# Batch 1's key-value products one block of w_out later, its v released later, its first q transposes one block sooner, and half of batch 2's maximum tree moved into tile 1

## The chip, the cores and the metric

The kernel runs on one core of one Trainium2 chip. A core has TensorE (PE in the profile; its weight loads are listed apart as PEld), VectorE (DVE), ScalarE (ACT), GpSimd (POOL) and SyncE (SP), which here only issues DMAs. Each engine works through its own instructions in order; engines wait for one another, and for DMAs, on semaphores. The metric is the device time of one execution in microseconds (us). Lower is better.

## The reference, cut to what matters

```python
# q, k, v: (8 batches, 8 heads, 576 positions, 64); float32
q_s = exp(q - max(q, axis=-1));  q_s /= sum(q_s, axis=-1)      # over the head's 64
k_s = exp(k - max(k, axis=2));   k_s /= sum(k_s, axis=2)       # over the 576 positions
kv  = einsum('bhsd,bhse->bhde', k_s, v)                        # 64x64 for each head
x   = einsum('bhsd,bhde->bhse', q_s, kv)                       # then to (4608 tokens, 512)
h   = x @ w_in                                                 # 512 -> 2048
out = maximum(0.01 * h, h) @ w_out                             # 2048 -> 512
```

There is no product of q with k: attention here is two softmaxes and two small products. Nearly all the arithmetic lies in the two dense layers behind it.

## The kernel before

**Tiles.** The 4608 tokens are cut into nine tiles of 512 columns. `xT` holds the attention's result, channels on partitions, tokens along columns. A batch has 576 tokens, so tile 0 needs batch 0 alone, and tile 1 needs the last 64 tokens of batch 0 and the first 448 of batch 1, and so on. In each tile layer 1 (`layer1`, L511) makes 16 blocks `ph` of 128 hidden channels, ScalarE applies the leaky rectifier to each (`leaky`, L520, into `gj`), and layer 2 (`layer2`, L532) accumulates 16 products into each of four `pout` blocks, which are copied to `out_sb` and stored by SP (L526, L529). In tile 0 layer 2 goes block of w_out by block of w_out: for each j of 16, four matmuls, one for each of the four 128-token groups. In later tiles it goes token group by token group.

**The attention of the next batches lies between these matmuls.** The order is written by hand. `at(t, u, fns)` hangs functions on hook u of tile t; `run(t, u)` emits them there. In tile 0, hooks 0 to 31 come in pairs behind the leaky rectifiers of layer 1, and hook 32 + j comes behind the four layer-2 matmuls of w_out block j. In a later tile, hook j comes behind the rectifier of block j, and hook 16 + 4g + i behind the fourth, eighth, twelfth and sixteenth matmul of token group g. A hook settles where an instruction stands in its own engine's queue and nothing more; between engines only the semaphores count.

**One batch's steps**, each with its line in the profile:

- k: a maximum over the nine positions that a partition holds, in four steps on VectorE (`k_tree`, L151; H0 and H1 are the two halves of the four head rows); the maximum over partitions by transposes on VectorE (`k_allmax`, L156 to L176); the subtraction (`k_sub`, L184); the exponential on ScalarE into `ke` (`k_exp`, L192).
- v: a cast to bf16 `vb` (`v_cast`, L202 on ScalarE, L204 on GpSimd).
- q: maximum (L215), subtraction (L274, on GpSimd or VectorE), exponential on ScalarE (L282), sum, reciprocal and scaling on VectorE (L291, L293, L298). Batch 1's q is turned by transposes on TensorE, seven positions of one half at a time (`q_turn_first`, L254, into `psum_q`), and ScalarE copies each to `qT` (`q_keep_first`, L267). From batch 2 on a DMA turns it (`q_turn`, L504).
- the 72 small matmuls of k with v (`kv`, L311, into two `pkv` buffers), their scaling on VectorE (`kd_make`, L330 and L331, into `kd`), and the product of q with the result (`cross`, L430, into `po`), which is copied into `xT` (L453, L499 for batch 1's `attend_next`).

**PSUM.** One pool, `psB`, has six buffers, and `ph`, `pkv`, `psum_q`, `psum_qt`, `po` and two of tile 0's four `pout` blocks share them. A new tile takes a buffer that is free in program order, and its first matmul waits for the last reader of the old one.

**Loads.** SP issues all loads of q, k and v, in program order, and waits on semaphores in that order too. Two small devices hold it back. `hold_sync` (L563) loads a few bytes from a weight, so that what SP issues later comes behind that weight's landing. In `more_loads` ScalarE writes one element into batch 1's v tile (L637), so that SP may issue the load of v only once ScalarE has come that far. The weights w_in and w_out are loaded from GpSimd's queue, w_out's blocks 2 to 15 in seven pieces.

```python
    def more_loads():
        st[1]["v"] = t = raw("v_raw")
        nc.scalar.copy(out=t[0:1, 0, 0, 0:1], in_=identf[0:1, 0:1])
        load(v, 1, "v_raw", [(H0, ALLR), (H1, ALLR)], t)
        hold_sync(1, w_out_sb[0:1, 11, 0:128])
```

Of the kernel before, what the change touches and what calls it, by code (L numbers as in the profile page):

```python
# [25 lines left out]
def kernel(  # L26
# [9 lines left out]
    nc = tc.nc  # L36
# [95 lines left out]
    def k_begin(b):  # L132
        st[b]["ke"] = ke_pool.tile([P, R, HL, D], BF16, name="ke")
        st[b]["kmax"] = mx_pool.tile([P, HL, D], FP32, name="kmax")
        st[b]["kmaxT"] = mx_pool.tile([P, HL * D], FP32, name="kmaxT")
        st[b]["kall"] = mx_pool.tile([P, HL, D], FP32, name="kall")

    def k_tree(b, hs, steps=slice(0, 4)):
        n = hs.stop - hs.start
        ks = st[b]["k"][:, hs]  # L140
        if steps.start == 0:
            st[b]["t4"] = mx_pool.tile([P, HL, 4, D], FP32, name="t4")[:, 0:n]
        t4 = st[b]["t4"]
        t2, t1 = t4[:, :, 0:2], t4[:, :, 0]
        for o, i0, i1 in (
            (t4, ks[:, :, 0:4], ks[:, :, 4:8]),
            (t2, t2, t4[:, :, 2:4]),
            (t1, t1, t4[:, :, 1]),
            (st[b]["kmax"][:, hs], t1, ks[:, :, 8]),
        )[steps]:  # L150
            nc.vector.tensor_tensor(out=o, in0=i0, in1=i1, op=ALU.max)  # L151
# [29 lines left out]
    def k_sub(eng, b, hs):  # L181
        ks = st[b]["k"][:, hs]
        n = hs.stop - hs.start
        eng.tensor_tensor(  # L184
            out=ks,
            in0=ks,
            in1=st[b]["kall"][:, hs].unsqueeze(2).to_broadcast([P, n, R, D]),
            op=ALU.subtract,
        )
# [17 lines left out]
    def q_begin(b):  # L207
        st[b]["qe"] = qe_pool.tile([P, R, HL, D], BF16, name="qe")
        if b < 2:
            st[b]["qT"] = qT_pool.tile([P, NB, R, L], BF16, name="qT", tag="qT")  # L210
# [39 lines left out]
    def q_turn_first(b, gg, rs=RA):  # L250
        n = rs.stop - rs.start
        ps = psB_pool.tile([P, 2, n, L], BF16, name="psum_q2", tag=BANK_TAG)
        for r in range(n):
            nc.tensor.matmul(  # L254
                ps[:, :, r],
                lhsT=st[b]["qe"][:, rs.start + r, 2 * gg : 2 * gg + 2].rearrange("p h d -> p (h d)"),
                rhs=ident,
                is_transpose=True,
                start=(r == 0),
                stop=(r == n - 1),  # L260
            )
        st[b]["ps2", gg] = ps

    def q_keep_first(eng, b, gg, rs=RA):
        o, i = st[b]["qT"][:, gg::2, rs], st[b]["ps2", gg]
        if eng is nc.scalar:
            eng.copy(out=o, in_=i)  # L267
        else:
            eng.tensor_copy(out=o, in_=i)
# [11 lines left out]
    def q_exp(b, rs, hs=ALLH):  # L281
        nc.scalar.activation(  # L282
            out=st[b]["qe"][:, rs, hs].rearrange("p r h d -> p h r d"),
            in_=st[b]["q"][:, hs, rs],
            func=AF.Exp,
        )

    def q_sum(b, rs, hs=ALLH):
        n, m = rs.stop - rs.start, hs.stop - hs.start
        qsum = small_pool.tile([P, n, HL], FP32, name="qsum")[:, :, 0:m]  # L290
        nc.vector.reduce_sum(out=qsum, in_=st[b]["qe"][:, rs, hs], axis=AX.X)  # L291
        st[b]["qrec", rs.start, hs.start] = qrec = small_pool.tile([P, n, HL], FP32, name="qrec")[:, :, 0:m]
        nc.vector.reciprocal(out=qrec, in_=qsum)  # L293

    def q_norm(b, rs, hs=ALLH):
        n, m = rs.stop - rs.start, hs.stop - hs.start
        qes = st[b]["qe"][:, rs, hs]
        nc.vector.tensor_tensor(  # L298
            out=qes,
            in0=qes,  # L300
            in1=st[b]["qrec", rs.start, hs.start].unsqueeze(3).to_broadcast([P, n, m, D]),
            op=ALU.mult,
        )


    def kv_quads(b, gg, outs, rs=ALLR):
        for r in range(R)[rs]:
            for hp in range(2):
                for hh in range(2):
                    rows = slice(hh * L, (hh + 1) * L)  # L310
                    nc.tensor.matmul(  # L311
                        outs[hh][hp * D : (hp + 1) * D, 0 : D + 1],
                        lhsT=st[b]["ke"][rows, r, 2 * gg + hp],
                        rhs=vb2[b % 2][rows, r, gg, hp, 0 : D + 1],
                        start=(r == 0),
                        stop=(r == R - 1),
                    )

    def kv(b, order=(0, 1)):

        pkv = [psB_pool.tile([P, 2, D + 2], FP32, name="pkv", tag=BANK_TAG) for _ in range(2)]
        for gg in order:
            kv_quads(b, gg, [pkv[hh][:, gg] for hh in range(2)])
        st[b]["pkv"] = pkv

    def kd_make(b):
        for hh in range(2):
            pkv = st[b]["pkv"][hh]
            krec = small_pool.tile([P, 2, 1], FP32, name="krec")
            nc.vector.reciprocal(out=krec, in_=pkv[:, :, D : D + 1])  # L330
            nc.vector.tensor_tensor(  # L331
                out=kd2[b % 2][:, :, hh],
                in0=pkv[:, :, 0:D],
                in1=krec.to_broadcast([P, 2, D]),
                op=ALU.mult,
            )
# [62 lines left out]
    def q_transpose(b, r0, n, pool=psB_pool, tag=BANK_TAG):  # L399
        ps = pool.tile([P, NB, n, L], BF16, name="psum_qt", tag=tag)  # L400
        for rr in range(n):
            for gg in range(2):
                nc.tensor.matmul(  # L403
                    ps[:, gg::2, rr],
                    lhsT=st[b]["qe"][:, r0 + rr, 2 * gg : 2 * gg + 2].rearrange(
                        "p h d -> p (h d)"
                    ),
                    rhs=ident,
                    is_transpose=True,
                    start=(rr == 0 and gg == 0),  # L410
                    stop=(rr == n - 1 and gg == 1),
                )
        st[b]["ps", r0] = ps

    def q_keep(eng, b, r0, n, gs=slice(0, 4)):
        o, i = st[b]["qT"][:, gs, r0 : r0 + n], st[b]["ps", r0][:, gs]
        if eng is nc.scalar:
            eng.copy(out=o, in_=i)
        else:
            eng.tensor_copy(out=o, in_=i)  # L420
# [122 lines left out]
    def at(t, u, *fns):  # L543
        while t > 0 and u >= 32:
            t, u = t + 1, u - 32
        hooks.setdefault((t, u), []).extend(fns)
# [5 lines left out]
    H0, H1 = slice(0, 2), slice(2, 4)  # L552
# [74 lines left out]
    R7, RE = slice(0, 7), slice(7, R)  # L627
# [21 lines left out]
    at(0, 20, lambda: q_max(1, R7, H0), lambda: q_sub(nc.gpsimd, 1, R7, H0), lambda: k_allmax(1))  # L649
    at(0, 20, lambda: q_max(1, R7, H1), lambda: q_sub(nc.gpsimd, 1, R7, H1), lambda: k_sub(nc.vector, 1, H1))  # L650
    at(0, 20, lambda: k_sub(nc.gpsimd, 1, H0))
    at(0, 25, more_loads)
    at(0, 31, lambda: q_exp(1, R7, H0), lambda: q_sum(1, R7, H0), lambda: q_norm(1, R7, H0))
    at(0, 31, lambda: k_exp(1, H1))
    at(0, 32, lambda: q_exp(1, R7, H1), lambda: q_sum(1, R7, H1), lambda: q_norm(1, R7, H1))
    at(0, 32, lambda: q_sum(0, R3), lambda: q_norm(0, R3))
    at(0, 32, lambda: v_cast(nc.scalar, 1, 0), lambda: v_cast(nc.scalar, 1, 1), lambda: k_exp(1, H0))
    at(0, 42, lambda: q_turn_first(1, 0, R7), lambda: q_keep_first(nc.scalar, 1, 0, R7))
    at(0, 43, lambda: kv(1, (1, 0)), lambda: kd_make(1))
    at(0, 44, lambda: q_turn_first(1, 1, R7), lambda: q_keep_first(nc.scalar, 1, 1, R7))  # L660
    at(0, 44, lambda: q_transpose(0, 8, 1), lambda: q_keep(nc.scalar, 0, 8, 1))
    at(0, 45, lambda: k_begin(2), lambda: q_begin(2), lambda: k_tree(2, H0))
    at(0, 46, attend_next)
    at(1, 0, lambda: q_max(1, RE), lambda: q_sub(nc.gpsimd, 1, RE))
    at(1, 5, lambda: q_exp(1, RE))
# [4 lines left out]

    def plan2():
        b = 2
        at(1, 0, lambda: k_tree(b, H1))
        at(1, 3, lambda: q_max(b, XR[0]), lambda: q_sub(nc.gpsimd, b, XR[0]))
        at(1, 3, lambda: k_allmax(b), lambda: k_sub(nc.vector, b, H0), lambda: k_sub(nc.vector, b, H1))
        at(1, 6, lambda: q_max(b, XR[1]), lambda: q_sub(nc.gpsimd, b, XR[1]))
        at(1, 11, lambda: q_exp(b, XR[0]), lambda: q_sum(b, XR[0]), lambda: q_norm(b, XR[0]))
        at(1, 13, lambda: v_cast(nc.gpsimd, b, 0), lambda: v_cast(nc.gpsimd, b, 1))
        at(1, 14, lambda: q_sum(1, RE), lambda: q_norm(1, RE))
        at(1, 15, lambda: k_exp(b, ALLH), lambda: q_turn(b, XR[0]))  # L680
        at(1, 16, lambda: q_exp(b, XR[1]), lambda: q_sum(b, XR[1]), lambda: q_norm(b, XR[1]))
        at(1, 17, lambda: q_turn(b, XR[1]))
        at(1, 17, lambda: load_all(4))
        at(1, 23, lambda: kv(b))
        at(1, 24, lambda: kd_make(b))
        at(1, 27, lambda: attend_all(b, (XR[0],)), lambda: attend_all(1, (RE,)))
        at(2, 19, lambda: attend_all(b, (XR[1],)))
# [28 lines left out]
    for t in range(3, B - 1):  # L716
        b = t + 1
# [140 lines left out]
```

## Time and profile before

| what | value |
|---|---|
| time, median of 3 runs | 283.06 us (282.93 to 283.38) |
| profiled execution: its own time | 282.68 us |
| profiled execution: span, first to last instruction | 280.9 us |
| granted TensorE clock | 0.998 |
| PE busy | 274.5 us, 98% of the span |
| ACT busy, DVE busy, POOL busy | 161.8, 159.3, 53.4 us |
| bytes moved by DMA | 45.81 MB, mean 163 GB/s |

How to read it: the span is what the engines' instructions cover; the profiled execution's own time has 1.8 us more around it. An engine's busy share over the span says little of a single stage. The chain that ended last tells which engine the end followed, and a timeline of one engine tells when each instruction began, how long it took and what ended an idle stretch before it. A PE row's duration is that of a pipelined instruction and reaches into the next one; the step from one matmul to the next is read from the chain of waits.

### The profile page before, as it was taken

To read this page: it belongs to the slowest core of one execution; us is meant where nothing else is said; L and a number is where in the kernel's file an instruction comes from. 1 tells how busy PE (TensorE), PEld (TensorE's weight loads), DVE (VectorE), ACT (ScalarE), POOL (GpSimd) and SP (SyncE) were. 2 spreads that over 40 slices of the span, in tenths; PEclk is the share of its full clock that TensorE was granted. 3 is DMA by queue.
4 is the path that set the end of the run, shared out by engine and by line. 5 is a ranking of instruction groups with operands and counts; after the bars stand their busy time and mean duration, and the time that the engine had idled before them with its cause. 6 is when DMAs were issued, how large, how long until landed. Compare 5 with 4: busy or idle time off the path is not lost.

```text
span 280.9 us, 5008 instructions
## 1 busy us (share of the span) xinstructions
PE 274.5 (98%) x2022; PEld 133.1 (47%) x2022; DVE 159.3 (57%) x225; ACT 161.8 (58%) x286; POOL 53.4 (19%) x52
## 2 busy tenths in 40 slices
PE   8899999999999999999999999999999999999994
PEld 2378645444444544444444444444444444444443
DVE  2975898999999939966895598644600000000021
ACT  4987575793589276755586448644844364146400
POOL 2847380457013006000400070000000000000000
PEclk9999999999999999999999999999999999999999
DMA  7999999895890696089309930333033300330033
GB/s 243 334 208 317 263 222 392 295 365 194 276 389 18 146 395 204 1 241 400 100 2 279 384 77 0 84 77 74 5 84 75 71 6 0 75 77 0 0 75 77
DMA packets 37207, 45.81 MB, mean 163 GB/s; under 512 B 16064, under 2 KB 20416, under 8 KB 37184
## 3 DMA queue, kind: packets, MB, share of 16 engines
q1 hardware_dynamic: 33696, 41.16, 45.9%
q0 software_dynamic: 3328, 4.20, 8.5%
q8 instruction: 16, 0.26, 0.4%
q10 hardware_dynamic: 160, 0.13, 0.1%
q14 instruction: 7, 0.06, 0.1%
HBM read 36.70 MB, written 9.44 MB: 164 GB/s over the span
## 4 chain that ended last, share of the span: by engine, by line
PE 92%; DVE 3%; DMA 2%; ACT 1%; issue 0%; SPq 0%
PE pout L532 45%; PE ph L511 43%; DMA k_raw<-in_k_dram 2%; PE po L430 2%; DVE t L151 1%; PE pokv L311 1%; PE pkv L311 1%; DVE qe L298 0%; DVE qsum L291 0%; DVE k_raw L380 0%; ACT vb L202 0%; PE psum_q L254 0%; ACT ke L192 0%; PE psum_qt L403 0%; ACT qe L282 0%
## 5 line engine op out<-in xcount | busy, mean ns | idle before, releaser
L532 PE MATMUL pout<-w_out_sb,gj 128*128 128x512 bf16 (+2 forms) x592 | 128.1, 373 | 0.0
L511 PE MATMUL ph<-xT,w_in_sb 128*128 128x512 bf16 (+1 forms) x640 | 126.7, 358 | 0.0
L520 ACT ACTIVATE gj<-ph 128x512 bf16<-128x512 f32 x144 | 82.2, 600 | 26.4 <-PE ph L511 26.1
L511 PEld LDWEIGHTS <-w_in_sb 128*128 128x128 bf16 x640 | 62.3, 98 | 62.2 <-issue 0.2
L532 PEld LDWEIGHTS <-gj 128*128 128x128 bf16 x592 | 56.4, 98 | 64.7 <-issue 0.2
L526 ACT COPY out_sb<-pout 128x512 f32<-128x512 f32 (+1 forms) x29 | 16.8, 579 | 66.0 <-PE pout L532 43.8
L526 DVE COPY out_sb<-pout 128x512 f32<-128x512 f32 (+1 forms) x8 | 4.8, 636 | 70.8 <-PE pout L532 70.8
L204 POOL CAST vb<-v_raw 128x1152 bf16<-128x1152 f32 x13 | 24.4, 1901 | 81.2 <-DMA v_raw<-in_v_dram 58.2
L291 DVE TENSOR_REDUCE qsum<-qe 128x36 f32<-128x2304 bf16 (+5 forms) x13 | 20.0, 1542 | 10.2 <-ACT qe L282 10.1
L192 ACT ACTIVATE ke<-k_raw 128x2304 bf16<-128x2304 f32 (+2 forms) x11 | 17.6, 1597 | 9.5 <-DVE k_raw L184 9.4
L298 DVE TENSOR_TENSOR qe<-qe,qrec 128x2304 bf16<-128x2304 bf16 (+5 forms) x13 | 22.4, 1724 | 0.5
L215 DVE TENSOR_REDUCE qmax<-q_raw 128x36 f32<-128x2304 f32 (+5 forms) x13 | 20.0, 1536 | 0.7 <-DMA q_raw<-in_q_dram 0.7
L282 ACT ACTIVATE qe<-q_raw 128x2304 bf16<-128x2304 f32 (+5 forms) x13 | 17.1, 1317 | 2.4 <-POOL q_raw L274 2.4
L184 DVE TENSOR_TENSOR k_raw<-k_raw,kall 128x2304 f32<-128x2304 f32 (+1 forms) x8 | 17.2, 2163 | 0.3
L453 ACT CAST xT<-po 128x512 bf16<-128x512 f32 (+3 forms) x35 | 15.7, 536 | 1.6 <-PE po L430 1.6
L274 POOL TENSOR_TENSOR q_raw<-q_raw,qmax 128x512 f32<-128x512 f32 (+3 forms) x7 | 12.2, 1736 | 22.1 <-DMA q_raw<-in_q_dram 9.7
L151 DVE TENSOR_TENSOR t<-t 128x256 f32<-128x256 f32 (+2 forms) x22 | 14.7, 669 | 0.7
L151 DVE TENSOR_TENSOR t<-k_raw 128x512 f32<-128x512 f32 (+1 forms) x11 | 13.1, 1188 | 3.0 <-DMA k_raw<-in_k_dram 2.7
L330 DVE RECIPROCAL krec<-pokv 128x2 f32<-128x2 f32 x8 | 1.3, 165 | 22.1 <-PE pokv L430 22.1
L274 DVE TENSOR_TENSOR q_raw<-q_raw,qmax 128x2304 f32<-128x2304 f32 (+1 forms) x6 | 13.2, 2203 | 0.6 <-issue 0.5
L342 PE MATMUL pout<-zero 128*128 128x512 bf16 x24 | 8.8, 510 | 1.3 <-POOL zero L99 1.3
L311 PEld LDWEIGHTS <-ke 64*64 64x64 bf16 x576 | 6.7, 107 | 4.2 <-issue 2.5
(65 smaller groups left out, 107.0 us busy)
## 6 DMA issues: line engine op xcount, KB each, us to landing
out_dram<-out_sb SPq DMA_DIRECT2D x70, 128.0 KB, 2.6
q_raw<-in_q_dram SPq DMA_DIRECT2D x6, 1152.0 KB, 8.4
v_raw<-in_v_dram SPq DMA_DIRECT2D x6, 1152.0 KB, 11.2
k_raw<-in_k_dram SPq DMA_DIRECT2D x5, 1152.0 KB, 6.1
k_raw<-in_k_dram SPq DMA_DIRECT2D x6, 576.0 KB, 6.0
v_raw<-in_v_dram SPq DMA_DIRECT2D x4, 576.0 KB, 7.7
w_in_sb<-in_moe_w_in_dram POOLq DMA_DIRECT2D x8, 256.0 KB, 7.4
w_out_sb<-in_moe_w_out_dram POOLq DMA_DIRECT2D x8, 256.0 KB, 11.6
```

The lines of the kernel that those rows point to most:

```text
L151: nc.vector.tensor_tensor(out=o, in0=i0, in1=i1, op=ALU.max)
L184: eng.tensor_tensor(out=ks, in0=ks, in1=st[b]["kall"][:, hs].unsqueeze(2).to_broadcast([P, n, R, D]), op=ALU.subtract,)
L192: nc.scalar.activation(out=st[b]["ke"][:, :, hs].rearrange("p r h d -> p h r d"), in_=st[b]["k"][:, hs], func=AF.Exp,)
L204: eng.tensor_copy(out=o, in_=i)
L215: nc.vector.tensor_reduce(out=o, in_=st[b]["q"][:, hs, rs], axis=AX.X, op=ALU.max)
L274: eng.tensor_tensor(out=qs, in0=qs, in1=st[b]["qmax", rs.start, hs.start].unsqueeze(3).to_broadcast([P, m, n, D]), op=ALU.subtract,)
L291: nc.vector.reduce_sum(out=qsum, in_=st[b]["qe"][:, rs, hs], axis=AX.X)
L298: nc.vector.tensor_tensor(out=qes, in0=qes, in1=st[b]["qrec", rs.start, hs.start].unsqueeze(3).to_broadcast([P, n, m, D]), op=ALU.mult,)
L511: nc.tensor.matmul(ph, lhsT=w_in_sb[:, cb, j * P : (j + 1) * P], rhs=xT[:, cb, c0 : c0 + n], start=(cb == 0 and first), stop=(cb == NB - 1 ...
L520: nc.scalar.activation(out=o, in_=ph, func=AF.Prelu, alpha=LEAKY_SLOPE)
L526: copy(out=out_sb, in_=pout)
L532: nc.tensor.matmul(pout, lhsT=g_sb[j // 2][:, j % 2, tsub * P : (tsub + 1) * P], rhs=w_out_sb[:, j, os], start=(j == 0), stop=(j == NF - 1),)
```

## The change

Six lines of the plan change; no function does. The numbers in `at(0, 32 + j, ...)` are places behind w_out block j of tile 0.

- The hook of `more_loads` goes from 25 to 27, which is one pair of layer-1 blocks later in ScalarE's queue.
- `q_turn_first(1, 0, R7)`, the first transposes of batch 1's q with their copy, go from behind w_out block 10 to behind block 9.
- `kv(1, (1, 0))` and `kd_make(1)` go from behind block 11 to behind block 12, and there behind the second transposes and the one of batch 0's last position.
- `k_begin(2)`, `q_begin(2)` and `k_tree(2, H0)` go from behind block 13 of tile 0 to hook 0 of tile 1, behind batch 1's `q_max` and just ahead of `k_tree(2, H1)`.

```diff
-    at(0, 25, more_loads)
+    at(0, 27, more_loads)
...
-    at(0, 42, lambda: q_turn_first(1, 0, R7), lambda: q_keep_first(nc.scalar, 1, 0, R7))
-    at(0, 43, lambda: kv(1, (1, 0)), lambda: kd_make(1))
+    at(0, 41, lambda: q_turn_first(1, 0, R7), lambda: q_keep_first(nc.scalar, 1, 0, R7))
     at(0, 44, lambda: q_turn_first(1, 1, R7), lambda: q_keep_first(nc.scalar, 1, 1, R7))
-    at(0, 44, lambda: q_transpose(0, 8, 1), lambda: q_keep(nc.scalar, 0, 8, 1))
-    at(0, 45, lambda: k_begin(2), lambda: q_begin(2), lambda: k_tree(2, H0))
+    at(0, 44, lambda: q_transpose(0, 8, 1), lambda: kv(1, (1, 0)), lambda: q_keep(nc.scalar, 0, 8, 1), lambda: kd_make(1))
     at(0, 46, attend_next)
...
     def plan2():
         b = 2
-        at(1, 0, lambda: k_tree(b, H1))
+        at(1, 0, lambda: k_begin(b), lambda: q_begin(b), lambda: k_tree(b, H0), lambda: k_tree(b, H1))
```

The instructions of every engine stay the same in kind and number; SP's and GpSimd's keep their order.

## The prediction

> **What bounds the kernel.** I read the page's busy table first, then the chain of waits, then the timelines of ScalarE, SP, VectorE and TensorE around the four edits.
>
> ```profile
> PE 274.5 (98%) x2022; PEld 133.1 (47%) x2022; DVE 159.3 (57%) x225; ACT 161.8 (58%) x286; POOL 53.4 (19%) x52
> ```
>
> TensorE is busy for 98% of the span, and from 31.09 us to 277.15 us the chain of waits holds its matmuls alone. So a saving on another engine shortens nothing, and a wait that TensorE takes on in between lengthens the run by its full length. The chain over the stage that the change rearranges:
>
> ```profile
> 40.58 0.39 PE psum_q L254 x7
> 40.97 0.86 PE pout L532 x4
> 41.84 0.71 PE pkv L311 x70
> 42.55 0.97 PE pout L532 x4
> 43.52 0.39 PE psum_q L254 x7
> 43.91 0.11 PE psum_qt L403 x2
> 44.02 1.73 PE pout L532 x8
> 45.75 0.57 PE po L430 x16
> 46.31 0.97 PE pout L532 x4
> 47.28 13.81 PE ph L511 x64
> ```
>
> The last line gives the pace without a wait: 13.81 / 64 = 0.216 us a matmul, 0.863 for a block of four. All layer-2 pieces here keep it, but for 0.11 us more behind each group of small matmuls. So there is no stall to recover. What feeds this stage is ScalarE's queue, and ahead of it SP's load of batch 1's v:
>
> ```profile
> 29.00 0.17 ACT L637 COPY v_raw<-identf 1x1 f32<-1x1 f32 x1
> 29.38 0.60 ACT L520 ACTIVATE gj<-ph 128x512 bf16<-128x512 f32 x1 [0.21 <-PE ph L511]
> ...
> 39.70 1.15 ACT L202 CAST vb<-v_raw 128x1152 bf16<-128x1152 f32 x1 [0.28 <-DMA v_raw<-in_v_dram]
> 40.86 1.16 ACT L192 ACTIVATE ke<-k_raw 128x1152 bf16<-128x1152 f32 x1
> 41.93 0.89 ACT L267 COPY qT<-psum_q 128x896 bf16<-128x896 bf16 x1
> ```
>
> ```profile
> 29.20 0.89 SPq L81 DMA_DIRECT2D v_raw<-in_v_dram x2
> ```
>
> ScalarE waits for v's second half, which lands at 39.68 (the trace's DMA semaphores), and then cast, exponential and copy run without a pause. This is the one place in the stage where a DMA sets ScalarE's time. Then VectorE in tile 1:
>
> ```profile
> 44.24 0.69 DVE L151 TENSOR_TENSOR t<-k_raw 128x512 f32<-128x512 f32 x1 [0.65 <-DMA k_raw<-in_k_dram]
> ...
> 50.36 0.68 DVE L151 TENSOR_TENSOR t<-k_raw 128x512 f32<-128x512 f32 x1
> 51.08 1.47 DVE L151 TENSOR_TENSOR t<-t 128x256 f32<-128x256 f32 x2
> ...
> 70.01 0.29 DVE L331 TENSOR_TENSOR kd<-pkv,krec 128x128 bf16<-128x128 f32 x1
> ```
>
> From 47.38 to 98.57 that timeline shows no idle stretch before any group, so work added at 50 us is still late at 70 and at 98.
>
> **The change, part by part.** Times here are starts in the timelines (TensorE's starts lie some 0.1 to 0.2 us ahead of the chain's).
>
> *Order on TensorE.* The same matmuls, with as many changes between large and small ones. Block 10 starts at 39.56 before (40.42 less 0.863). After: first transposes at 39.56, blocks 10, 11 and 12 at 39.95, 40.81 and 41.67, second transposes at 42.54, the single transpose pair at 42.93, and with 0.11 for it and 0.09 for the switch (before: block 11 ends at 41.67, the small matmuls start at 41.77) the k-v products at 43.13. Block 13 then starts at 43.85; before it is 43.86. Cost 0. Needed inputs: the first scaled q half is done at 37.15 + 1.19 = 38.34, the second at 41.77, batch 0's last position at 42.79 against 42.93. All in time.
>
> *v released later.* The marker L637 goes behind one more rectifier; these are 0.875 apart (28.50, 29.38), so v is issued at 30.08. What the transfer then does is not shown by the trace of before. Bounds: it lands as before (0), or 0.87 later. By the DMA packets, v's first 2304-byte packets start at 32.79, 3.6 us behind its issue. The nearest row is the few bytes of the first hold, issued at 18.94 with the weights' queue full and SP's queue empty: first packet at 22.80, 3.9 us. The k load at 40.12, with the weights nearly done, took 1.2 us. With weights still moving until 42.13, v is like the first, so I take the whole 0.87. The weights gain what v loses early and lose it later: block 12's piece landed at 40.87 and is now wanted at 41.67. Cost 0 there.
>
> *The k-v products against ScalarE.* In the changed program's order with its waits, the second small matmul waits for the copy L267 of the first transposes: that copy frees the PSUM buffer that the second `pkv` takes. Before, `pkv` took other buffers, and only the single transpose, at 43.75, waited for the copy. The copy ends at 41.93 + 0.89 = 42.82; with v 0.87 later, 43.69. A wait on ScalarE ends 0.04 behind it (exponential done at 14.41, first k-v product at 14.46). So the products go on at 43.73 in place of 43.13: **a stall of 0.60 us**, between 0 (v lands as before: 42.86) and 0.60 plus what jitter of v adds. Nothing behind takes it back. `kd` follows 1.0 us behind the products (42.55 to 43.59), about 45.5, and `po` comes two blocks behind them, 46.3: no second wait. The second copy L267 and the small one (0.91 and 0.38) end at about 45.0: in time.
>
> *The maximum tree moved.* At 44.24 it sat in a stretch where VectorE has nothing else to do (the copies of `po` start only with `po`): removing it gains 0. It runs 1.8 us there (44.24 to 46.05). In tile 1 two such trees follow each other. One pays for the neighbour on GpSimd, as now (50.36 to 52.80, 2.44), the other costs 1.77 (the steps from 44.24 to 46.05, less the pause). VectorE's queue is then 1.77 late until it next idles (98.6). Who is behind it, with the times that TensorE needs, both without the 0.60 common to all:
> - `kd` of batch 2: 70.30 + 1.77 = 72.07, wanted by `po` at 72.45. Slack 0.38.
> - GpSimd's subtraction of batch 2's q and ScalarE's exponential behind it: 57.43 + 1.77 = 59.2, where the exponential now starts at 58.17; the last four rectifiers slip 1.05, to about 62.8, and layer 2 wants the last at 61.10 + 15 x 0.216 = 64.3. Hidden. The GpSimd casts of v end at 66.04 + 1.77 = 67.8; the second half is wanted at 68.3.
> - SP waits for the scaled q: the DMA transposes go out at 65.19 + 1.8, land 3.3 later at 70.3, wanted at 72.45. Behind them in SP's queue, batch 4's loads at 70.86 and the stores at 72.59 leave 1.8 later; k of batch 4 landed at 76.8 and is first read at 82.95. Hidden.
> - `ke` of batch 4, below: 97.80 + 2.12 + 1.77 = 101.69 with 0.04, wanted at 101.80. Slack 0.07.
>
> ```profile
> 97.80 2.12 ACT L192 ACTIVATE ke<-k_raw 128x2304 bf16<-128x2304 f32 x1 [2.46 <-DVE k_raw L184]
> ```
>
> ```profile
> 101.80 0.38 PE L311 MATMUL pokv<-vb,ke 64*64 64x65 bf16 x24
> ```
>
> I take 0 for the tree. Its upper bound is the contended 2.44 for both trees: 0.67 more than I take, which leaves stalls of 0.67 - 0.38 = 0.29 at `po` and of 0.67 - 0.07 - 0.29 = 0.31 more at `ke`, together 0.60. Its lower bound is 0, as it frees no wait of TensorE.
>
> *A rule weighed.* In the Trainium skill, "DMA: Bandwidth & Descriptors", section "Queues, rings and completion order", each DMA engine is said to go round-robin between the queues it has work for, packet by packet. By that rule v would start moving soon after its issue, at about 31.3 with the 1.2 us of the row of 40.12, so no later than now, and the sum would be 0 (R1 below); the trace's 32.79 and 22.80 speak against it for new work beside a full queue.
>
> **The sum.** 0 (order) + 0.60 (v and the buffer) + 0 (tree) = +0.60. The profiled execution's own time is 282.68, its span 280.9 and 1.8 around; it lies 0.38 under the median. 282.68 + 0.60 = 283.28 for such an execution, and with the same 0.38 **283.66** for the median. A measurement of this kernel can tell about 0.2% from no change, 0.57 us, so this is just over it.
>
> **The rivals.**
> *R1, v's landing doesn't move.* Two ways lead there. v started at 32.79 just as the last packets of q ended (32.51); if q's tail held it, an issue at 30.08 changes nothing. Or v moves 1.2 us behind its issue, as k at 40.12 did, so from 31.3. Then the copy ends at 42.82, the products start on time, and the time is 283.06, give or take the 0.15 of batch 2's waits. For it: the coincidence. Against it: the first hold waited 3.9 us with no q ahead of it, and v itself waited 3.6. The second way is what the rule of the Trainium skill above would give.
> *R2, faster.* Block 10 of layer 2 needs w_out's fifth late piece, landed at 39.49, and starts at 39.56: 0.07 us of room. If in most executions it lands later, before has a stall there that the profile doesn't show, and after, with the transposes ahead of that block, has 0.39 us more room. It decides from a landing 0.07 late, and gains up to 0.38, the distance of the median from the profiled execution: 282.68, provided v's landing does not move. Against it: the chain shows no wait there at all.
> *R3, the tree also counts.* The stall of 0.60, and 0.2 to 0.6 more at `po` or `ke` of batch 4: 283.9 to 284.3. For it: slacks of 0.38 and 0.07 under a queue without idle time. Against it: both slacks are positive as worked out.
>
> **Chances.** The forecast (0.40 to 0.80 over before: 283.45 to 283.85) 0.50, R1 0.20, R2 0.10, R3 0.20. The range leaves out about half of R2 at the bottom and the rare double mishap at the top: 282.75 to 284.40. Cases of both signs don't hold most of the chance. Faster by over 0.2% comes from R2: 0.09. Within 0.2%: R1, and the lower part of the forecast, 0.11: 0.31. Slower: the rest, 0.60.
>
> **What would show it.** Right: in the new profile the load of v issued near 30.1 and landed near 40.5; the copy L267 ending near 43.7; a gap of about 0.6 in the chain at the k-v products of tile 0; everything from tile 1 on 0.6 later; VectorE's `kd` of batch 2 about 0.4 us ahead of `po`. Wrong: v landing at 39.7 (R1), a profiled span at or under 280.9 (R2), or gaps in the chain at `po` near 72.5 or at `pokv` near 102 (R3). The forecast also fails if block 12's weights, wanted 0.87 earlier, arrive after 41.67.

## The result, and the profile after

The changed kernel takes 283.46 us in the median of 22 runs (283.12 to 283.88) where the kernel before takes 283.01 in the runs beside it. The ratio is 1.0014 with a 95% interval of 1.0007 to 1.0020: 0.45 us slower, within 0.2 and 0.57. So it is slower, and yet within the 0.2% that the prediction called no change. One of the 22 runs of the kernel before took 480.99 us; the ratio leaves it out, and without it that median is 283.00.

The busy table of the page of the changed kernel:

```profile
PE 272.3 (97%) x1994; PEld 133.2 (47%) x2022; DVE 159.4 (57%) x225; ACT 161.6 (57%) x286; POOL 50.8 (18%) x52
```

TensorE's work is the same; the count is lower because 28 matmul records are missing from this trace, and a missing one looks like a step that is longer by one matmul's 0.22 to 0.23, not like a wait. What has changed is the chain of waits. It was TensorE alone from 31 us on; now it leaves TensorE twice. In tile 0 (start, length, what, in us):

```profile
30.25 0.37 SPq L81
30.67 9.92 DMA v_raw<-in_v_dram
40.64 1.03 issue
41.67 1.16 ACT ke L192
42.83 0.80 ACT qT L267
43.67 0.77 PE pkv L311 x71
44.60 1.67 PE pout L532 x7
```

The load of v's second half (issued at 30.67, landed at 40.59), ScalarE's cast (the 1.03 of "issue" lies within it), its exponential and its copy of the first q transposes follow each other without a pause, and 71 of the 72 k-v products come behind that copy. The same stage in ScalarE's and TensorE's timelines:

```profile
40.61 1.16 ACT L202 CAST vb<-v_raw 128x1152 bf16<-128x1152 f32 x1 [1.07 <-DMA v_raw<-in_v_dram]
41.67 1.16 ACT L192 ACTIVATE ke<-k_raw 128x1152 bf16<-128x1152 f32 x1
42.74 1.69 ACT L267 COPY qT<-psum_q 128x896 bf16<-128x896 bf16 x2
```

```profile
43.11 0.27 PE L403 MATMUL psum_qt<-ident,qe 128*128 128x128 bf16 x2
43.32 1.12 PE L311 MATMUL pkv<-vb,ke 64*64 64x65 bf16 x72
```

ScalarE waited 1.07 for v where it waited 0.28 before. The first product starts at 43.32, the second at 43.67: a step of 0.36, where the first step was under 0.01 before and the largest of the 72 was 0.04. From the first start to the last the products take 0.93 us in place of 0.59: 0.34 us lost.

The second time the chain leaves TensorE at 46.69, with the copies of `po`, runs along VectorE's queue, and comes back in tile 2:

```profile
97.68 2.57 DVE k_raw L184
100.28 2.13 ACT ke L192
102.45 0.38 PE pokv L311 x24
```

VectorE, late by the tree, sets ScalarE's exponential of batch 4, and that ends at 102.40, when TensorE has just run out of layer-2 matmuls: the step from the last of them to the products is 0.44, and 0.31 before. Lost: 0.13 us. In between, tile 1's `po` does not wait, as VectorE's and TensorE's timelines show:

```profile
72.38 0.29 DVE L331 TENSOR_TENSOR kd<-pkv,krec 128x128 bf16<-128x128 f32 x1
```

```profile
72.97 0.52 PE L430 MATMUL po<-qX,kd 64*64 64x384 bf16 x8
```

`kd` ends at 72.67, 0.30 ahead of its use; it was 2.15 ahead before.

A profile's span also carries what happened ahead of the change. Layer 2 of tile 0 starts at 31.11 here and at 30.92 in the trace of before, because layer 1 waited at 19.9 for a piece of w_in; in the other profiles below it starts between 30.98 and 31.51 with no relation to the edit. So all traces are compared by one stretch: from the first layer-2 matmul of tile 0 to the first layer-1 matmul of tile 3. It lasts 106.49 - 30.92 = 75.57 before and 107.15 - 31.11 = 76.04 after: +0.47, of which 0.34 is at the k-v products and 0.13 at `pokv`. The medians differ by 0.45.

### The profile page after: what moved, and what is told of

It reads as the page before. It is cut to its first block, busy times and chain, and to the rows that moved or that the text cites. A ratio compares the mean times of both kernels' runs of the same rounds, so it can differ in the third digit from the quotient of the medians.

```text
span 281.6 us, 4979 instructions
## 1 busy us (share of the span) xinstructions
PE 272.3 (97%) x1994; PEld 133.2 (47%) x2022; DVE 159.4 (57%) x225; ACT 161.6 (57%) x286; POOL 50.8 (18%) x52
## 3 DMA queue, kind: packets, MB, share of 16 engines
HBM read 36.70 MB, written 9.44 MB: 164 GB/s over the span
## 4 chain that ended last, share of the span: by engine, by line
PE 66%; DVE 17%; DMA 9%; issue 2%; ACT 2%; POOL 2%; SPq 0%; DVEq 0%; ACTq 0%
PE ph L511 32%; PE pout L532 31%; DMA v_raw<-in_v_dram 4%; DVE t L151 3%; DMA w_in_sb<-in_moe_w_in_dram 3%; DVE qe L298 3%; DMA k_raw<-in_k_dram 2%; DVE qmax L215 2%; DVE k_raw L184 2%; DVE qsum L291 2%; ACT ke L192 1%; PE po L430 1%; PE pokv L311 1%; DVE out_sb L526 1%; DMA out_dram<-out_sb 1%
## 5 line engine op out<-in xcount | busy, mean ns | idle before, releaser
L532 PE MATMUL pout<-w_out_sb,gj 128*128 128x512 bf16 (+2 forms) x573 | 126.4, 373 | 1.2 <-issue 0.3
L204 POOL CAST vb<-v_raw 128x1152 bf16<-128x1152 f32 x13 | 21.7, 1701 | 82.1 <-DMA v_raw<-in_v_dram 82.1
L342 PE MATMUL pout<-zero 128*128 128x512 bf16 x23 | 7.7, 470 | 1.4 <-POOL zero L99 1.3
```

The lines of the kernel that those rows point to most:

```text
L532: nc.tensor.matmul(pout, lhsT=g_sb[j // 2][:, j % 2, tsub * P : (tsub + 1) * P], rhs=w_out_sb[:, j, os], start=(j == 0), stop=(j == NF - 1),)
```

## The experiments

Each ran beside the kernel before on the same chip, 4 to 12 runs against 21 to 30 of before; the chip is not the same for all rows. "Stretch" is the one just defined (75.57 in the trace of before).

| run | edit | median, us | before beside it | ratio, 95% interval | stretch over before |
|---|---|---|---|---|---|
| the change | | 283.46 | 283.01 | 1.0014 (1.0007 to 1.0020) | +0.47 |
| e1 | change, v released as before | 283.13 | 282.92 | 1.0006 (0.9997 to 1.0015) | +0.09 |
| e2 | change, tree as before | 283.31 | 282.92 | 1.0017 (1.0008 to 1.0026) | +0.46 |
| e3 | before, v released later | 283.49 | 282.92 | 1.0021 (1.0011 to 1.0031) | +0.63 |
| e4 | before, tree in tile 1 | 283.02 | 282.92 | 1.0007 (0.9998 to 1.0016) | +0.17 |
| e5 | change, copy ahead of the cast | 283.11 | 283.07 | 1.0000 (0.9991 to 1.0009) | +0.13 |
| e6 | order in tile 0 alone | 283.05 | 283.07 | 0.9998 (0.9989 to 1.0007) | +0.40 |
| e7 | change, v one pair later still | 284.12 | 283.07 | 1.0038 (1.0024 to 1.0052) | +1.29 |
| e8 | change, tree computed twice | 285.16 | 283.07 | 1.0078 (1.0063 to 1.0093) | +2.25 |
| e9 | before, first transposes sooner | 282.89 | 282.92 | 0.9991 (0.9981 to 1.0002) | +0.01 |
| e10 | e6 again | 282.90 | 282.92 | 0.9992 (0.9983 to 1.0001) | +0.07 |

### e1: v's release undone

```diff
-    at(0, 27, more_loads)
+    at(0, 25, more_loads)
```

> The change with the release of v put back (hook 25). Theory A (v's later landing moves the copy L267 of the first q transposes, and that copy holds the PSUM buffer of the second pkv; the tree in tile 1 adds a short wait for ke of batch 4): v lands near 39.7, the copy ends near 42.8, before the second k-v product needs its buffer (43.1 to 43.3), so the 0.33 us gap there goes and about 0.13 us at pokv stays: 0.1 to 0.2 us over before. Theory B (the new order of transposes and k-v products costs by itself, v's landing doesn't matter): the gap stays, 0.45 over before. Theory C (the tree alone costs): 0.45 over before, all of it at or behind tile 1's po.

v lands at 39.81, the copy ends at 42.86, and TensorE's timeline shows all 72 products in one group:

```profile
43.38 0.78 PE L311 MATMUL pkv<-vb,ke 64*64 64x65 bf16 x72
```

The gap is gone with one number changed, so the order alone does not make it. The time left over is 0.21 us with an interval that takes in zero. Theories B and C fall. The 0.13 us expected at `pokv` is not there: the step to it is 0.31, as before (e4 tells why).

### e2: the tree undone

```diff
+    at(0, 45, lambda: k_begin(2), lambda: q_begin(2), lambda: k_tree(2, H0))
...
-        at(1, 0, lambda: k_begin(b), lambda: q_begin(b), lambda: k_tree(b, H0), lambda: k_tree(b, H1))
+        at(1, 0, lambda: k_tree(b, H1))
```

> The change with batch 2's tree of H0 back in tile 0 behind w_out block 13. Theory A: the gap of about 0.33 us at tile 0's k-v products stays, the wait at pokv near 102 goes: 0.3 to 0.4 us over before. Theory B: the same, 0.45. Theory C: as before, 0.

0.39 us slower. The trace names the wait (the list of TensorE's waits):

```profile
PE pkv L311 <- ACT qT L267: 0.2, 1, 0.2
```

Its step is 0.42 (0.40 lost over the 72 products), and `pokv` follows its predecessor after 0.31, as before. So most of the cost stays when the tree is put back.

### e3: v's release alone, on the kernel before

```diff
-    at(0, 25, more_loads)
+    at(0, 27, more_loads)
```

> The kernel before with v released at hook 27 and nothing else changed. Theory A: the exponential that feeds the second half of the k-v products ends at 42.02 + 0.87 = 42.89 where TensorE wants it at 42.07: a gap of 0.75 to 0.82 inside the 72 products of tile 0, 0.75 us over before, more than the whole change costs. Theory B: v's landing doesn't matter, 0. Theory C: 0.

Chain of waits of e3:

```profile
41.90 1.17 ACT ke L192
43.07 0.04 issue
43.11 0.48 PE pkv L311 x36
```

Here the second half of the products waits for the exponential itself: a step of 0.65, and 0.63 lost over the 72 products. The kernel is 0.57 us slower by the medians, where the whole change costs 0.45; the intervals overlap, so by time it is not shown to cost more. By these profiles the products' move by a block takes back 0.3 of what the later release costs (0.63 against 0.34).

### e4: the tree alone, on the kernel before

```diff
-    at(0, 45, lambda: k_begin(2), lambda: q_begin(2), lambda: k_tree(2, H0))
...
-        at(1, 0, lambda: k_tree(b, H1))
+        at(1, 0, lambda: k_begin(b), lambda: q_begin(b), lambda: k_tree(b, H0), lambda: k_tree(b, H1))
```

> The kernel before with the tree of H0 in tile 1 and nothing else changed. Theory A: VectorE is 1.77 us late from 52 to 98 us; kd of batch 2 is still in time for po, ke of batch 4 is 0.1 late for pokv: 0.1 to 0.2 over before. Theory B: 0. Theory C: 0.45.

ScalarE's and TensorE's timelines:

```profile
99.96 2.12 ACT L192 ACTIVATE ke<-k_raw 128x2304 bf16<-128x2304 f32 x1 [4.45 <-DVE k_raw L184]
```

```profile
102.14 0.38 PE L311 MATMUL pokv<-vb,ke 64*64 64x65 bf16 x24
```

The exponential ends at 102.08 and the products start 0.06 behind it, 0.47 after the last layer-2 matmul: 0.16 lost, all of it there. By time alone (+0.10, interval through zero) it could not be told from nothing; it is the trace that shows it, here, after the change and in e5 (0.13 each), while e1's exponential came just in time.

What sets e1 apart is batch 4's own maximum tree, which VectorE runs beside GpSimd's cast of v. VectorE's and GpSimd's timelines, first of e1, then of e4:

```profile
85.03 1.22 DVE L151 TENSOR_TENSOR t<-k_raw 128x1024 f32<-128x1024 f32 x1
85.13 3.66 POOL L204 CAST vb<-v_raw 128x1152 bf16<-128x1152 f32 x2 [14.37 <-DMA v_raw<-in_v_dram]
```

```profile
84.96 2.19 DVE L151 TENSOR_TENSOR t<-k_raw 128x1024 f32<-128x1024 f32 x1
84.93 3.23 POOL L204 CAST vb<-v_raw 128x1152 bf16<-128x1152 f32 x2 [14.23 <-DMA v_raw<-in_v_dram]
```

Where VectorE began first, its first step took 1.22 us and the whole tree 4.50 (e1; 4.52 before the change, where it was first by 0.04). Where GpSimd began first, they took 2.19 and 4.66 (e4; 2.17 and 4.63 after the change). This difference of 0.11 to 0.16 us is enough to decide whether `ke` comes in time. No run varied the cast alone.

### e5: the copy in ScalarE's waiting time

```diff
-    at(0, 32, lambda: v_cast(nc.scalar, 1, 0), lambda: v_cast(nc.scalar, 1, 1), lambda: k_exp(1, H0))
-    at(0, 41, lambda: q_turn_first(1, 0, R7), lambda: q_keep_first(nc.scalar, 1, 0, R7))
+    at(0, 32, lambda: v_cast(nc.scalar, 1, 0))
+    at(0, 40, lambda: q_turn_first(1, 0, R7), lambda: q_keep_first(nc.scalar, 1, 0, R7))
+    at(0, 40, lambda: v_cast(nc.scalar, 1, 1), lambda: k_exp(1, H0))
```

> The change with v released late as in it, but the first q transposes one more block sooner (behind block 8) and their copy L267 ahead of the cast of v's second half in ScalarE's queue, where ScalarE waits for v anyway. Theory A (the copy holds the second pkv's buffer): the copy ends near 40.3, long before the k-v products, and the gap between their first and second matmul goes though v lands as late as in the change; what stays is the tree's wait at pokv: 0.1 to 0.2 us over before. Theory D (the products wait for v's own cast or exponential): the exponential ends as before near 42.8, or up to 0.2 later, so the gap would stay: 0.45 over before.

ScalarE's and TensorE's timelines:

```profile
39.60 0.91 ACT L267 COPY qT<-psum_q 128x896 bf16<-128x896 bf16 x1
40.71 1.15 ACT L202 CAST vb<-v_raw 128x1152 bf16<-128x1152 f32 x1 [0.20 <-DMA v_raw<-in_v_dram]
41.76 1.16 ACT L192 ACTIVATE ke<-k_raw 128x1152 bf16<-128x1152 f32 x1
```

```profile
43.45 0.78 PE L311 MATMUL pkv<-vb,ke 64*64 64x65 bf16 x72
```

v lands as late as in the change (40.68), cast and exponential run as late, and the gap is gone. So it was the copy, as holder of the buffer, that the products waited for, and neither v nor the exponential. Theory D falls. The time is that of before within 0.25 us.

### e6 and e10: the order alone

```diff
-    at(0, 27, more_loads)
+    at(0, 25, more_loads)
+    at(0, 45, lambda: k_begin(2), lambda: q_begin(2), lambda: k_tree(2, H0))
...
-        at(1, 0, lambda: k_begin(b), lambda: q_begin(b), lambda: k_tree(b, H0), lambda: k_tree(b, H1))
+        at(1, 0, lambda: k_tree(b, H1))
```

> The order in tile 0 alone: transposes and k-v products as in the change, v's release and the tree as before. Theory A: no wait anywhere, 0 against before (within 0.1). Theory B (the order costs by itself): 0.2 to 0.45 over before. If before has a hidden wait for w_out's fifth late piece at block 10, this kernel has 0.39 us more room there and would be 0.1 to 0.3 faster.

The time is that of before, but this profile has waits of TensorE that the one of before has not: 0.11 at block 8 of layer 2 in tile 0, whose w_out piece landed at 37.97, and 0.31 in two at tile 1's first layer-1 matmuls. VectorE's timeline of e6:

```profile
45.20 0.69 DVE L151 TENSOR_TENSOR t<-k_raw 128x512 f32<-128x512 f32 x1
45.92 0.75 DVE L151 TENSOR_TENSOR t<-t 128x256 f32<-128x256 f32 x2
46.71 0.29 DVE L151 TENSOR_TENSOR kmax<-t,k_raw 128x128 f32<-128x128 f32 x1
46.92 1.28 DVE L499 CAST xT<-po 128x512 bf16<-128x512 f32 x2
```

With `kd` later, the tree that stays in tile 0 runs up to the copies of `po`, which tile 1 reads first. If that were so in every execution, the tree's move would have a use that the prediction denied it. So it ran once more:

> The order in tile 0 alone a second time, to see whether the waits of 0.15 and 0.17 at tile 1's first layer-1 matmuls, which its first profile shows, come again. Theory A, amended (kd comes 1.5 us later, so the tree of H0 in tile 0 starts behind kd at 45.1 and the copies of po into xT start behind the tree at 46.9): the same waits within 0.15, 0.2 to 0.4 at tile 1, and a time 0 to 0.3 over before. If they came from a late landing of batch 2's k in that one execution alone: no such waits, 0.

The second profile has no such waits. Batch 2's k landed at 44.34 there and at 45.17 in e6, so the tree started at 44.92 and not at 45.20, and the copies at 46.64 and not at 46.92. The amended theory falls as a rule: by these two profiles it takes a late landing of k. The order alone costs nothing that these runs can tell.

### e7: v released one pair later still

```diff
-    at(0, 27, more_loads)
+    at(0, 29, more_loads)
```

> The change with v released one pair of layer-1 blocks later still (hook 29). Theory A: v, copy and the gap at the k-v products all move by 0.87: a gap near 1.2 us, 1.3 over before. If the transfer's start were tied to something else than the issue, the gap would stay near 0.33 and the time near the change's.

Chain of waits of e7:

```profile
31.49 9.85 DMA v_raw<-in_v_dram
...
43.59 0.80 ACT qT L267
44.39 0.04 issue
44.43 0.77 PE pkv L311 x71
```

The step is 1.08, and 1.07 are lost over the 72 products. Counted from the start of layer 2, v is issued 0.87 later than after the change, and v's landing, the copy's end and tile 1's first matmul are each 0.81 later (0.08 of the last is lost ahead of the first product, as the transposes L403 had to wait for their scaled q). So the cost goes with the release, nearly one for one, as it must if v sets the copy. The total of 1.05 is some 0.25 under what was expected.

### e8: the tree computed twice

```diff
-        at(1, 0, lambda: k_begin(b), lambda: q_begin(b), lambda: k_tree(b, H0), lambda: k_tree(b, H1))
+        at(1, 0, lambda: k_begin(b), lambda: q_begin(b), lambda: k_tree(b, H0), lambda: k_tree(b, H0), lambda: k_tree(b, H1))
```

> The change with the tree of H0 computed twice in a row in tile 1 (the same result). VectorE is 1.8 us later again. Theory A: kd of batch 2 ends near 74.4 and po of tile 1 waits about 1.5 us; ke of batch 4 ends near 104.2 and pokv waits 0.2 to 0.3 more: 1.75 over the change, 2.2 over before. If VectorE had slack that the timelines hide, less than 1.

2.09 us over before; the stretch is 1.78 longer than the change's, close to the 1.83 that the added tree takes. So VectorE's queue in tiles 1 and 2 has no hidden room behind the change. But the wait came elsewhere. TensorE's timeline:

```profile
68.80 0.48 PE L311 MATMUL pkv<-vb,ke 64*64 64x65 bf16 x36
70.17 0.48 PE L311 MATMUL pkv<-vb,ke 64*64 64x65 bf16 x36 [0.89 <-POOL vb L204]
```

It is not `po` that waits for `kd`, as was expected: the k-v products of batch 2 lose 1.07 to GpSimd's cast of v, which stands behind GpSimd's subtraction of q, which waits for VectorE's maximum. Before that, layer 2 waits 0.46 for the last rectifiers (64.5 to 65.0), and at `pokv` another 0.2 more than after the change. For the change the prediction had put the cast's end at 67.8 against 68.3 and the rectifiers at 62.8 against 64.3, and so gave both more room than `kd` (0.38). With one more tree it was not `kd` that was late first.

### e9: the first transposes alone

```diff
-    at(0, 42, lambda: q_turn_first(1, 0, R7), lambda: q_keep_first(nc.scalar, 1, 0, R7))
+    at(0, 41, lambda: q_turn_first(1, 0, R7), lambda: q_keep_first(nc.scalar, 1, 0, R7))
```

> The kernel before with the first q transposes behind block 9 and nothing else changed. Theory A: no wait before, none after: 0 (within 0.1). Theory E (most executions of before wait at block 10 for w_out's fifth late piece): 0.1 to 0.3 faster.

0.9991 with an interval through 1: no gain that can be told from none. Neither it nor the order alone is shown to beat the kernel before.

## Why the prediction was right, and where it wasn't

*The mechanism was right.* Of the four edits v's later release costs most, and by the path that was forecast: through ScalarE's queue to the copy that holds the second `pkv`'s buffer. e1 and e5 each take out one link of that path and the gap goes; e2 takes out the tree and the gap stays; e7 releases v later still and the gap grows. e3 shows that without the new order the later release costs through another wait.

*Order on TensorE: right to the hundredth.* Products expected 43.13 - 30.92 = 12.21 us behind the start of layer 2; measured 43.32 - 31.11 = 12.21. Cost expected 0; e10 shows 0.07 in the stretch and no slower time.

*v's landing: right in the main.* It was expected near 40.5 and measured at 40.59. Counted from the start of layer 2, which came 0.19 later in this trace, it moved by 0.73 of the 0.87 that were taken. Part of that is chance: in the six profiles with v released at hook 25 it lands 8.58 to 8.76 us behind that start, before the change the latest of them, and in the five with hook 27 9.44 to 9.54; the means are 0.83 apart. By the DMA packets, v's first packet comes 3.58 us behind its issue after the change and 3.60 before. R1 falls twice: in e7, v's first packet (34.64) comes 2.0 us behind q's last (32.62), so q's tail is not what holds it; and v never goes out 1.2 us behind its issue. With that falls, for this stage, the prompt start that the prediction drew from the round-robin of the Trainium skill's "DMA: Bandwidth & Descriptors" (section "Queues, rings and completion order"): the trace has 3.6 us.

*The stall: right in place and cause, wrong in size.* Step of the prediction: "the products go on at 43.73 in place of 43.13: a stall of 0.60 us". Measured 0.34 (after) and 0.40 (e2). Counted from the start of layer 2, the copy was put at 43.69 - 30.92 = 12.77 and ended at 43.62 - 31.11 = 12.51. Of the missing 0.26, 0.15 is v: it landed 9.48 behind that start, not 9.63, since first packet to landing took 6.76 in place of 6.89. And 0.11 is a second wait that the prediction overlooked: from landing to the copy's end it took 3.13 us before and 3.03 after. GpSimd's timeline, before and after:

```profile
37.35 3.47 POOL L184 TENSOR_TENSOR k_raw<-k_raw,kall 128x1152 f32<-128x1152 f32 x1
```

```profile
37.48 3.47 POOL L184 TENSOR_TENSOR k_raw<-k_raw,kall 128x1152 f32<-128x1152 f32 x1
```

The exponential reads what this subtraction writes. Before, the subtraction ended at 40.82 and the exponential began at 40.86, 1.16 behind the cast; in e1, e4, e6, e9 and e10 too it began 0.03 behind the subtraction's end. After, the subtraction ended at 40.95 and the exponential began at 41.67, 1.06 behind the cast. So the prediction's reading that cast, exponential and copy ran without a pause behind v was wrong by 0.10 us: by so much v could be late for nothing. e3's loss came out short in the same way, 0.63 for an expected 0.75 to 0.82.

*The tree: 0 was taken, 0.13 is right.* The slack of `ke` of batch 4 was put at 0.07 and is about -0.13. The term that was too small is VectorE's lateness of 1.77: the two trees of batch 2 take 4.28 us where the one took 2.44, which is 1.84, and batch 4's tree, with GpSimd first, takes 0.11 more. That part of R3 happened, while its stall at `po` did not (0.30 of room, 0.38 expected).

*R2 (faster) did not happen.* Block 10 had a wait neither before nor after, and e9, which alone tests it, shows no gain beyond its interval. A late piece of w_out can cost, as e6's profile shows at block 8, but of the twelve profiles only that one has such a wait.

*The sum.* 0.34 + 0.13 = 0.47 in the traces where 0.60 + 0 was forecast. 283.66 was forecast and 283.46 measured, which is 0.01 inside the range of 283.45 to 283.85. That it lies inside is luck: the two misses have opposite signs, and with the stall alone it would lie below. The outcome that was given the most weight, slower by over 0.2%, was missed by the size of the stall.

## What to carry to other kernels

Where one engine is busy all the time, ask of each edit which wait it gives that engine, and count the PSUM buffer that a new tile takes, with its last reader, as one of its inputs: here the products waited for a copy whose data they don't use. Where an instruction begins right behind one event, ask whether a second input came just as late: only one of them moves with the edit. A load that is released later moves everything that is queued behind its consumer, and work that doesn't need it can be put into the time in which that engine waits. When an engine's queue has no idle time for 50 us, a piece of 1.8 us put into it is felt at the far end, and the row to look at is the consumer with the least room, on whichever engine.

## What the runs showed of the hardware

In all twelve profiles the first packet of v's load comes 3.53 to 3.62 us behind its issue, wherever that lies between 29.20 and 31.07, while w_out's loads from GpSimd's queue are on the way. A load of the same shape at about 40.2, near the end of those loads, takes 1.2 us (1.16 to 1.19 in the seven of those profiles in which SP's queue had no other packets of that size in flight). The few bytes of the first hold are different: they are issued between 18.55 and 20.05 and always start at 22.5 to 22.9, in all twelve between the landing of the last piece of w_in but one and that of the last (21.8 and 23.0 in the trace of before). There the start does not move with the issue. The prediction took the one for the model of the other and came out right by the number alone. What makes the 3.6 us was not tried and stays open.
